# RWKV-5 attention and a SwiGLU block on one core: part of the input loads begun by ScalarE instead of SyncE

## The chip, the core and the metric

The kernel runs on one core of a Trainium2 chip. The metric is the time of one execution on the device in microseconds (us). The engines are called PE (TensorE, with PEld for its weight loads), DVE (VectorE), ACT (ScalarE), POOL (GpSimd) and SP (SyncE). SP computes nothing here: it begins transfers (DMAs). ACT computes, and it can begin transfers too; a transfer that an engine begins stands in that engine's instruction stream, in order with the rest of it. Such an instruction is called an issue below; the time at which all its data have arrived is its landing.

## What is computed

Inputs are r, k, v of shape (4 batches, 8 heads, 768 steps, 48), w and u of shape (8, 48), and the weights of the second part in float64, which the kernel reads as pairs of 32-bit words and rounds itself. All else is float32.

```python
for t in range(S):                                   # first part, by batch and head
    kt, vt, rt = (k[:, :, t], v[:, :, t], r[:, :, t])
    cur = np.einsum('bhd,bhe->bhde', u[None] * kt, vt)
    y[:, :, t] = np.einsum('bhd,bhde->bhe', rt, state + cur)
    state = w[None, :, :, None] * state + np.einsum('bhd,bhe->bhde', kt, vt)
x = y.transpose(0, 2, 1, 3).reshape(B * S, H * D)    # (3072, 384)
g = x @ w_gate                                       # w_gate, w_val: (384, 1536)
out = (g * (1.0 / (1.0 + np.exp(-g))) * (x @ w_val)) @ w_out
```

## The kernel before

**Units.** The first part is cut into 24 units, each worth 128 steps of all 8 heads. Units 0 to 7 are 128 steps of one batch; from unit 8 (`PAIRED`) on a unit holds 64 steps of each of two batches, in the two halves of the partitions. A loop over s runs unit s+1's preparation, unit s-1's scores and unit s-2's outputs side by side, and fills the gaps with matmuls of the second part (`feed`). Per unit: `load` brings k and r (two DMAs, four from unit 8 on, L147), `load_v` brings v (L153); POOL scales k and r and forms their product (L353, L356, L264, L267); unit 8 and later move 32-wide blocks inside SBUF with eight DMAs of SP (`move_blocks`, L435), which DVE transposes (L457); PE makes the scores (L496, later L548); DVE copies them under a mask into the tile At (L504, later L556); ACT writes the diagonal (L384, later L376 into a side tile that two of ACT's own DMAs bring into At, `fill_own`, L532); SP brings the transposed r there too (`fill_turned`, L526). PE multiplies At by v (L647, later L582) and ACT copies the result to xT (L651, later L586).

**Weights.** `chunks` lists 18 pieces of the weights, 0 to 17, in this text called chunks: 0 to 11 take turns between w_gate and w_val, 12 to 17 are w_out. `load_weights` (L184) begins the load of the next one into `w_bits`, a ring of three buffers of 768 KB. A chunk is then rounded to float32, by ACT (two L204 and one L210, in the order L204, L210, L204), DVE (L219 and L220 twice) and POOL (L252). `round_second` ends a chunk's rounding on ACT and begins a load, so that chunk n+2's load is written down right behind chunk n's rounding. PE uses rounded gate and value weights for units 0 to 3 while the rest is still being rounded (L690; ACT's L696 and DVE's L697 take its results from two PSUM banks); w_out must be complete before the first projection (L770). Later PE works on sums of weights that POOL forms (L862, L889, L959).

**Order.** The framework keeps each engine's instructions in the order in which the kernel writes them. It gives each transfer begun by SP or ACT one of eight completion counters, DMAHW0 to DMAHW7, in turn, both engines' transfers in one sequence; a transfer waits, before it is issued, for the landing of the last one that had its counter, which is the eighth before it in that sequence. Where the two are on different engines, one engine's stream stands until the other's transfer has landed.

Of the kernel before, what the change touches and what calls it, by code (L numbers as in the profile page):

```python
# [22 lines left out]
def fast(  # L23
# [25 lines left out]
    B, H, S, D = r.shape  # L49
# [15 lines left out]
    dve, pool, act, pe, sp = nc.vector, nc.gpsimd, nc.scalar, nc.tensor, nc.sync  # L65
# [63 lines left out]
    PAIRED = 8  # L129
# [6 lines left out]
    def pieces_of(i):  # L136

        if i < PAIRED:
            c, b = divmod(i, B)
            return [(slice(0, P), b, P * c)]  # L140
        return [(slice(64 * p, 64 * p + 64), *part(i, p)) for p in range(2)]
# [7 lines left out]
    def load_v(i):  # L149
        for rows, b, t in pieces_of(i):  # L150
            n = rows.stop - rows.start
            for e in range(2):
                sp.dma_start(  # L153
                    out=v_ld[b][rows, :, 64 * e : 64 * e + D],
                    in_=v[b, :, t : t + n, :].rearrange("(a e) t d -> e t a d", e=2)[e],
                )
# [17 lines left out]
    def next_chunk(stage):  # L174
        n = done[stage]
        done[stage] = min(n + 1, NW)
        return n if n < NW else None

    def load_weights():
        n = next_chunk("load")  # L180
        if n is not None:
            src = chunks[n][0].bitcast(INT32)
            bits[n] = three.tile([P, WN, 2], INT32, name="w_bits", tag="w_bits")
            sp.dma_start(  # L184
                out=bits[n][:].rearrange("p (c f) two -> p c (f two)", c=src.shape[1]), in_=src
            )

# [47 lines left out]
    def round_second(n):  # L235
        round_high(n, 1, 1)
        round_dve(n, 1)
        del bits[n]
        load_weights()
# [54 lines left out]
    load(0)  # L294
    load(1)
    load_weights()
    load_weights()
    load_v(0)
    load_v(1)

    act.activation(sg0[:], ident[:, 0:1], AF.Silu)
# [25 lines left out]
    for l in range(7):  # L327
        n = 1 << l
# [1054 lines left out]
    load(3)  # L1383
    load_weights()
    load_v(2)
    load_v(3)
    scores(0)
# [162 lines left out]
    n = nc.values_load(outside, min_val=0, max_val=512)  # L1550
# [416 lines left out]
```

## Time and profile before

| | |
|---|---|
| median of 3 runs | 609.83 us (606.59 to 610.46) |
| the profiled execution | 608.74 us, of which its span is 606.9 us |
| PE busy | 571.4 us, 94% of the span |
| DVE, POOL, ACT busy | 434.1, 393.2 and 221.2 us |
| moved by DMA | 51.26 MB |
| mean granted PE clock | 0.977 of full speed |

The span is what the profile's times count from; 1.8 us of the execution lie outside it. The chain of waits is read back from the last instruction: each row is the work that released the next. A row of the timeline gives start, duration, engine and line, and in brackets how long the engine stood idle before and what ended that; "SPq" and "ACTq" mark an issue in the stream of SP or ACT. A row of the waits gives the total, how often, and the longest.

### The profile page before, as it was taken

What the parts mean: (1) busy time and instruction counts of PE and PEld (TensorE: products, weight loads), DVE (VectorE), ACT (ScalarE), POOL (GpSimd) and SP (SyncE); (2) the same over time, 40 slices, a digit from 0 to 9 for tenths busy, and PEclk for the clock granted to TensorE, in tenths of its full rate; (3) what the DMA queues carried; (4) which work ended last, traced back from release to release, by engine and by line L of the source; (5) the groups of instructions that cost most, each with busy time, mean ns of one, the idle gap of its engine ahead of it and who ended that gap; (6) DMA issues with size and microseconds to landing.
All of it is one profiled execution on the core that took longest, in us unless ns stands there. A gap on an engine that the chain in (4) does not pass through costs nothing.

```text
span 606.9 us, 13839 instructions
## 1 busy us (share of the span) xinstructions
PE 571.4 (94%) x5450; PEld 513.8 (85%) x5450; DVE 434.1 (72%) x766; ACT 221.2 (36%) x528; POOL 393.2 (65%) x394
## 2 busy tenths in 40 slices
PE   8899959396999999999999999999999999999997
PEld 6788847285997889998889998889988889988896
DVE  7977666348748787959778959769728779367682
ACT  4669654221134443134452135441133331133320
POOL 5898756468699983797963797952998980001520
PEclk9999978599999999999999999999999999999999
DMA  7997968466354332564441564241110000200002
GB/s 194 222 261 207 230 198 157 114 123 106 65 116 78 71 65 45 91 138 74 81 78 32 115 124 73 44 75 29 28 27 0 1 2 1 53 0 2 1 2 56
DMA packets 161912, 51.26 MB, mean 84 GB/s; under 512 B 148465, under 2 KB 151538, under 8 KB 161842
## 3 DMA queue, kind: packets, MB, share of 16 engines
q1 hardware_dynamic: 156690, 42.79, 34.0%
q10 hardware_dynamic: 5152, 7.54, 4.9%
q8 instruction: 44, 0.72, 0.5%
q14 instruction: 26, 0.21, 0.1%
HBM read 28.31 MB, written 4.72 MB: 54 GB/s over the span
## 4 chain that ended last, share of the span: by engine, by line
PE 75%; DMA 7%; POOL 7%; SPq 3%; DVE 2%; issue 2%; ACT 2%; POOLq 0%; DVEq 0%; ACTq 0%
PE bank L959 28%; PE bank L770 14%; PE ring L959 13%; PE bank L1192 8%; PE bank L690 5%; DMA w_bits<-in_moe_w_out_dram 4%; POOL wgv L862 3%; PE ring L582 3%; POOL s L889 2%; PE ring L548 1%; DMA v_ld<-in_v_dram 1%; PE ring L1192 1%; PE ring L647 1%; DMA w_bits<-in_moe_w_val_dram 1%; PE ring L596 1%
## 5 line engine op out<-in xcount | busy, mean ns | idle before, releaser
L983 DVE TENSOR_TENSOR hv<-hv,bank 128x512 f32<-128x512 f32 x132 | 87.8, 683 | 37.5 <-PE bank L959 31.8
L690 PE MATMUL bank<-xT,wgv 128*128 128x256 f32 x288 | 69.3, 398 | 6.9 <-DVE hv L697 6.9
L690 PEld LDWEIGHTS bank<-xT,wgv 128*128 128x128 f32 x288 | 55.8, 198 | 16.1 <-DVE hv L697 7.3
L959 PE MATMUL bank<-xf,wgv 128*128 128x256 f32 x256 | 65.6, 381 | 0.0
L983 ACT COPY hv<-bank 128x512 f32<-128x512 f32 x72 | 40.8, 585 | 61.8 <-PE bank L959 54.4
L959 PEld LDWEIGHTS bank<-xf,wgv 128*128 128x128 f32 x256 | 48.1, 190 | 6.8 <-DVE kT L1237 0.6
L1246 POOL TENSOR_TENSOR hv<-At,hats 128x512 f32<-128x512 f32 x8 | 10.2, 1275 | 64.0 <-ACT At L1245 64.0
L376 ACT ACTIVATE zs<-mask,du 128x64 f32<-128x64 f32 x128 | 38.8, 345 | 26.4 <-DVE du L275 10.4
L990 ACT ACTIVATE hv<-hv 128x512 f32<-128x512 f32 (+2 forms) x36 | 22.8, 634 | 50.2 <-DVE hv L983 50.2
L770 PE MATMUL bank<-wt,hs 128*128 128x192 f32 x192 | 35.5, 338 | 4.1 <-DVE hs L744 4.1
L615 POOL TENSOR_TENSOR v_ld<-v_ld,w 48x384 f32<-48x384 f32 x28 | 24.4, 871 | 19.1 <-DVE v_ld L612 16.0
L770 PEld LDWEIGHTS bank<-wt,hs 128*128 128x128 f32 x192 | 32.9, 197 | 4.5 <-POOL rk L267 4.3
L959 PE MATMUL bank<-xT,wgv 128*128 128x256 f32 x144 | 35.6, 380 | 0.0
L959 PE MATMUL bank<-xT,s 128*128 128x256 f32 x152 | 35.4, 381 | 0.0
L889 POOL TENSOR_TENSOR s<-wgv 128x256 f32<-128x256 f32 x39 | 29.9, 787 | 7.3 <-PE bank L770 7.3
L770 PE MATMUL bank<-wo,hv 128*128 128x192 f32 x192 | 32.9, 327 | 1.7 <-DVE hv L697 1.7
L770 PE MATMUL bank<-wo,hs 128*128 128x192 f32 x192 | 34.0, 327 | 0.0
L770 PEld LDWEIGHTS bank<-wo,hv 128*128 128x128 f32 x192 | 31.5, 190 | 2.4 <-DVE hv L697 2.0
L959 PEld LDWEIGHTS bank<-xT,s 128*128 128x128 f32 x152 | 28.5, 190 | 4.8 <-issue 1.1
L747 POOL TENSOR_TENSOR hs<-hv,hs 128x768 f32<-128x768 f32 x6 | 11.3, 1876 | 32.1 <-DVE hs L744 32.1
L889 POOL TENSOR_TENSOR s<-s,wgv 128x256 f32<-128x256 f32 x39 | 30.2, 774 | 2.8
L889 POOL TENSOR_TENSOR s<-s 128x256 f32<-128x256 f32 x39 | 31.5, 806 | 0.8
(237 smaller groups left out, 1424.3 us busy)
## 6 DMA issues: line engine op xcount, KB each, us to landing
hats<-hats SPq DMA_DIRECT2D x128, 64.0 KB, 2.3
w_bits<-in_moe_w_gate_dram SPq DMA_DIRECT2D x6, 768.0 KB, 6.4
w_bits<-in_moe_w_val_dram SPq DMA_DIRECT2D x6, 768.0 KB, 7.2
w_bits<-in_moe_w_out_dram SPq DMA_DIRECT2D x6, 768.0 KB, 6.0
At<-zs ACTq DMA_DIRECT2D x32, 128.0 KB, 3.3
At<-rT SPq DMA_DIRECT2D x32, 128.0 KB, 2.4
k_ld<-in_k_dram SPq DMA_DIRECT2D x32, 96.0 KB, 3.3
r_ld<-in_r_dram SPq DMA_DIRECT2D x32, 96.0 KB, 3.1
```

The source lines that it names most:

```text
L376: lambda h=h: act.activation(own[:, i % 2, slot(i, h), :], ident64, AF.Identity, scale=du[:, h : h + 1])
L582: pe.matmul(ps[32 * q : 32 * q + 32, cc, 64 * p : 64 * p + 64], *x, start=start, stop=stop, skip_group_check=True,)
L615: pool.tensor_mul(ze, ze, w.unsqueeze(3).to_broadcast([D, HP, 2, D]))
L690: pe.matmul(gv[:, o, :].rearrange("p (i t) -> p i t", i=2), wt[:, c, P * f : P * (f + 1)], xT[:, 2 * g % NX : 2 * g % NX + 2, c, :], start ...
L747: on.tensor_sub(s[1], h12, x["s"][1])
L770: pe.matmul(ps, lhs[:, f, :], rhs[:, f, :], start=(f == 0 and n in (0, 1, 4)), stop=(f == FH - 1), skip_group_check=True,)
L862: lambda o=o, x=x, op=op: op(o, o, x) for o, x, op in ((w[1][1], w[0][1], pool.tensor_add), (w[1][1], w[1][2], pool.tensor_sub), (w[0][0], ...
L889: op(made[o], made[a], made[b])
L959: pe.matmul(ps[:, o], u[:, o], v, start=first and o == 0, stop=True, skip_group_check=True,)
L983: do(out, *(pair_of(wide[a][:]) if isinstance(a, str) else a for a in args))
L990: todo.append((at, lambda: act.activation(gate, gate, AF.Silu)))
L1192: pe.matmul(ps, (h[what][q] if h[what] is D_ else h[what][:, q])[:, f, :], wide["o"][what][:, f, :], start=first and f == 0 and (split or ...
```

## The change

Two lines change which engine begins a transfer. Chunk 5 and later are loaded by ACT (`n < 5` stays on SP; chunk 5 is the sixth), and so is v for units 8 to 11. What is moved, to where and how much stays the same.

```diff
@@ -150,7 +150,7 @@
         for rows, b, t in pieces_of(i):
             n = rows.stop - rows.start
             for e in range(2):
-                sp.dma_start(
+                (act if PAIRED <= i < PAIRED + B else sp).dma_start(
                     out=v_ld[b][rows, :, 64 * e : 64 * e + D],
                     in_=v[b, :, t : t + n, :].rearrange("(a e) t d -> e t a d", e=2)[e],
                 )
@@ -181,7 +181,7 @@
         if n is not None:
             src = chunks[n][0].bitcast(INT32)
             bits[n] = three.tile([P, WN, 2], INT32, name="w_bits", tag="w_bits")
-            sp.dma_start(
+            (sp if n < 5 else act).dma_start(
                 out=bits[n][:].rearrange("p (c f) two -> p c (f two)", c=src.shape[1]), in_=src
             )
```

So 13 issues of weights and 16 of v (four for each of four units) leave SP's stream and stand in ACT's. The orders of PE, DVE and POOL do not change.

ACT, from the end of chunk 4's rounding (rows of before with -, of the change with +, and in brackets the counters that a row waits for):

```order
+L184 DMA w_bits<-in_moe_w_gate_dram 128x3x512 [waits DMAHW7_49,Activation_49]
 L409 COPY kT_112<-ring_96 128x512 [waits PE_49]
 L409 COPY rT<-ring_97 128x512 [waits PE_49]
-L204 ACTIVATE bank_94<-w_bits 128x384 [waits DMAHW4_49,DVE_49]
-L210 ACTIVATE w_low<-w_bits 128x768 [waits Pool_49]
-L204 ACTIVATE bank_95<-w_bits 128x384 [waits DVE_49]
+L204 ACTIVATE bank_94<-w_bits 128x384 [waits DVE_49]
+L210 ACTIVATE w_low<-w_bits 128x768 [waits Pool_49]
+L204 ACTIVATE bank_95<-w_bits 128x384 [waits DVE_49]
+L184 DMA w_bits<-in_moe_w_val_dram 128x3x512 [waits DMAHW4_49,Activation_49]
 L696 ACTIVATE sgs<-bank_92 128x256 [waits PE_49]
 L384 ACTIVATE At_110<-ident,du 128x128 x3
```

The loads of chunks 6 and 7 now stand behind the rounding of chunks 4 and 5, and ACT's next work stands behind the loads. Chunk 7's load has counter DMAHW4, whose last user before it is on SP. There, in the changed kernel, stand the loads of k and r for unit 7 (k_ld_104, r_ld_102):

```order
L153 DMA v_ld_106<-in_v_dram 128x4x48 [waits DMAHW1_49,PE_49]
L153 DMA v_ld_106<-in_v_dram 128x4x48 [waits DMAHW2_49,PE_49]
L147 DMA k_ld_104<-in_k_dram 128x8x48 [waits DMAHW3_49,Pool_49]
L147 DMA r_ld_102<-in_r_dram 128x8x48 [waits DMAHW4_49]
L1464 DMA w_82<-w_82 64x4x1 [waits DMAHW5_49]
L1464 DMA w_82<-w_82 64x4x1 [waits DMAHW6_49]
```

So ACT's load of chunk 7 waits until r of unit 7 has landed; in the kernel before, that load stood on SP behind r's issue.

SP before, where it begins the load of the last chunk, 17 (the only L184 here), between the loads of k and r for unit 11 and those of v for unit 9:

```order
L147 DMA k_ld_104<-in_k_dram 64x8x48 [waits DMAHW3_49]
L147 DMA k_ld_104<-in_k_dram 64x8x48 [waits DMAHW4_49]
L147 DMA r_ld_102<-in_r_dram 64x8x48 [waits DMAHW5_49]
L147 DMA r_ld_102<-in_r_dram 64x8x48 [waits DMAHW6_49]
L184 DMA w_bits<-in_moe_w_out_dram 128x2x768 [waits DMAHW7_49,Activation_49]
L677 DMA v_ld_108<-zs 48x4x48 [waits DMAHW0_49,PE_49,Pool_49]
L677 DMA v_ld_108<-zs 48x4x48 [waits DMAHW1_49,PE_49,Pool_49]
L153 DMA v_ld_107<-in_v_dram 64x4x48 [waits DMAHW2_49]
```

In the changed kernel the L184 and the L153 are gone from this place. The chunk's load now stands on ACT behind chunk 15's rounding, with counter DMAHW2. ACT in the changed kernel, from chunk 16's rounding on (v_ld_107 and v_ld_108 are the v of unit 9):

```order
L204 ACTIVATE bank_94<-w_bits 128x384 [waits DMAHW6_49,DVE_49]
L210 ACTIVATE w_low<-w_bits 128x768 [waits Pool_49]
L204 ACTIVATE bank_95<-w_bits 128x384 [waits DVE_49]
L376 ACTIVATE zs<-mask,du 128x64 x2
L651 COPY xT<-ring_96 128x384 [waits PE_49]
L532 DMA At_111<-zs 64x512 [waits DMAHW7_49,Activation_49]
L532 DMA At_111<-zs 64x512 [waits DMAHW0_49]
L153 DMA v_ld_107<-in_v_dram 64x4x48 [waits DMAHW2_49]
L153 DMA v_ld_107<-in_v_dram 64x4x48 [waits DMAHW3_49]
L153 DMA v_ld_108<-in_v_dram 64x4x48 [waits DMAHW5_49,PE_49]
L153 DMA v_ld_108<-in_v_dram 64x4x48 [waits DMAHW6_49,PE_49]
L696 ACTIVATE sgs<-bank_92 128x256 [waits PE_49]
```

Before, the L696 stood right behind the two L532. Now the four issues of v stand between them, and the first of these, which has DMAHW2 too, waits until chunk 17 has landed.

## The prediction

> **What bounds the kernel now.** First the span, then stages of it, since the change touches only the first 140 us. In a row of stages stand the bounds and the length, each engine's busy us, the granted PE clock, the share in which DMA engines were busy, and GB/s.
>
> ```profile
> span 606.9 us, 13839 instructions
> ...
> core 0: us, PE busy (x) PEld busy (x) DVE busy (x) ACT busy (x) POOL busy (x), PEclk, DMA share, GB/s
> 36.00:58.00 22.00, 22.00 (x214) 19.17 (x213) 16.54 (x35) 18.98 (x48) 19.93 (x18) 1.00 0.91 230
> 58.00:82.00 24.00, 23.81 (x291) 20.34 (x289) 14.96 (x31) 14.21 (x34) 18.92 (x17) 1.00 0.85 202
> 82.00:117.00 35.00, 17.08 (x198) 14.03 (x202) 20.90 (x42) 17.81 (x49) 16.66 (x15) 0.73 0.63 153
> 117.00:133.00 16.00, 15.18 (x276) 13.08 (x268) 6.05 (x14) 4.01 (x13) 11.17 (x8) 0.85 0.68 128
> ...
> 150.00:194.00 44.00, 43.23 (x462) 39.97 (x461) 31.11 (x55) 11.19 (x31) 36.66 (x45) 0.97 0.43 86
> ```
>
> PE is full from 36 to 82 and again from 150 on. Between 82 and 117 it works 17.08 of 35.00 us. So **no engine bounds that stage; a chain of waits does**. The longest waits of PE and one of SP's stream (total, count, longest), then the chain of waits there:
>
> ```profile
> PE ring L582 <- DVE At L556: 11.2, 1, 11.2
> PE bank L690 <- DVE hv L697: 6.9, 1, 6.9
> ...
> SPq L147 <- DMA At<-zs: 13.0, 5, 5.5
> ```
>
> ```profile
> 91.50 5.92 DMA w_bits<-in_moe_w_out_dram
> ...
> 99.81 2.92 DMA At<-zs
> 102.75 0.65 SPq L147
> ...
> 104.12 0.63 SPq L147
> 104.85 6.63 DMA w_bits<-in_moe_w_out_dram
> ...
> 115.97 0.45 DVE At L556
> 116.46 0.55 PE ring L582 x12
> ```
>
> PE's longest wait ends at 116.46 (that for L697 lies ahead of it in the same stage). Read backwards: L582 waits for the mask copy At (DVE, 115.97). Ahead of it stands chunk 17's rounding, which waits for that chunk's load. The load was issued only at 104.85, because SP was standing before k of unit 11 (102.75), which needed a counter from ACT's At<-zs (99.81 + 2.92 = 102.73). SP stood 13.0 us in five such places. ACT's own timeline shows the other end:
>
> ```profile
> 94.78 0.52 ACT L204 ACTIVATE bank<-w_bits 128x384 f32<-128x384 f32 x1
> ...
> 97.50 0.54 ACT L204 ACTIVATE bank<-w_bits 128x384 f32<-128x384 f32 x1 [1.18 <-DMA w_bits<-in_moe_w_out_dram]
> ...
> 99.81 1.18 ACTq L532 DMA_DIRECT2D At<-zs  x2
> 101.04 0.38 ACT L696 ACTIVATE sgs<-bank 128x256 f32<-128x256 f32 x1 [0.89 <-ACT xT L651]
> 103.17 0.83 ACT L376 ACTIVATE zs<-mask,du 128x64 f32<-128x64 f32 x3 [1.74 <-DVE du L275]
> 111.50 0.51 ACT L204 ACTIVATE bank<-w_bits 128x384 f32<-128x384 f32 x1 [7.50 <-DMA w_bits<-in_moe_w_out_dram]
> ```
>
> Chunk 15's rounding ends at 95.30 (94.78 + 0.52), and behind it stands chunk 17's load in the changed kernel: 9.5 us earlier than 104.85. Chunk 17 is rounded at 111.50, after 7.50 us of standing, and PE resumes 4.96 us later.
>
> **Prices.** Issues on SP, what two issues cost ACT (the bracket of 101.04), and landings:
>
> ```profile
> 41.19 0.57 SPq L147 DMA_DIRECT2D r_ld<-in_r_dram  x1
> ...
> 67.12 1.32 SPq L147 DMA_DIRECT2D r_ld<-in_r_dram  x2
> ...
> 104.85 0.57 SPq L184 DMA_DIRECT2D w_bits<-in_moe_w_out_dram  x1
> ...
> 127.70 2.64 SPq L153 DMA_DIRECT2D v_ld<-in_v_dram  x4
> ...
> 130.43 1.23 SPq L526 DMA_DIRECT2D At<-rT  x2
> ```
>
> ```profile
> DMA to landing us min/median/max: 5.1/6.4/7.6
> ```
>
> ```profile
> DMA to landing us min/median/max: 2.6/3.2/6.6
> ```
>
> The first landing row is L184 in the whole trace, the second L147. ACT has no row of a weight load. Its two L532, 1.18 us of issue, held the next instruction 0.89 us, 0.45 each; its computing rows overlap by about 0.1 us. So a load costs ACT between nothing (under a wait) and 0.57; I take **0.3**, and **2.6** for four v issues (2.64 on SP). A load's landing on ACT's queue is bounded by 5.1 and 7.6; I take **5.6**, between the least and the 5.92 of chunk 16, which had fewer transfers around it than the median of 6.4.
>
> **The change, step by step.** Shifts are times after minus before.
>
> *Chunk 7's load (36 to 58).* It takes the counter of r of unit 7, so ACT waits for a landing of SP.
>
> ```profile
> DMA to landing us min/median/max: 5.7/5.8/5.9
> ```
>
> These are the k and r loads issued about 35, in the same traffic. 41.19 + 5.8 = 47.0, against 43.1 where chunk 5's rounding ends; with 0.3 and the overlap, L696 of 42.99 comes at 47.4: +4.4. By the median of 3.2 it would be 44.4 + 0.3, by the 6.6 it would be 47.8 + 0.3, so +1.7 to +5.1. ACT idles later:
>
> ```profile
> 42.99 0.38 ACT L696 ACTIVATE sgs<-bank 128x256 f32<-128x256 f32 x1
> ...
> 50.12 0.53 ACT L204 ACTIVATE bank<-w_bits 128x384 f32<-128x384 f32 x1 [0.53 <-DVE wgv L220]
> ...
> 58.62 0.38 ACT L696 ACTIVATE sgs<-bank 128x256 f32<-128x256 f32 x1 [0.78 <-PE bank L690]
> ...
> 65.77 0.54 ACT L204 ACTIVATE bank<-w_bits 128x384 f32<-128x384 f32 x1 [2.08 <-DMA w_bits<-in_moe_w_gate_dram]
> ...
> 69.10 0.53 ACT L204 ACTIVATE bank<-w_bits 128x384 f32<-128x384 f32 x1 [0.58 <-DMA w_bits<-in_moe_w_val_dram]
> ...
> 82.30 0.51 ACT L204 ACTIVATE bank<-w_bits 128x384 f32<-128x384 f32 x1 [4.61 <-DMA w_bits<-in_moe_w_out_dram]
> 87.79 0.38 ACT L696 ACTIVATE sgs<-bank 128x256 f32<-128x256 f32 x1 [0.89 <-ACT xT L651]
> ```
>
> 4.4 less 0.53, 0.78 and 2.08, plus 0.3 for each of four loads (chunks 8 to 11), is +2.2 at chunk 10's rounding (68.0); less 0.58, plus a load, +1.9 at chunk 11's (71.0). PE reads L696's bank and may stop some 2 us in this stage. I count that at nothing: PE idles 17.9 of the 35.00 us from 82 on, where this work can stand. Without that cover it would be +2.
>
> *Chunk 13's load.* It takes the counter of the first r half of unit 10, issued at 67.12. SP is some 4.4 late there, as its stream waits for counters of ACT's loads: 71.5 + 3.2 = 74.7, landing 80.3. Chunk 13 is rounded at 80.3 instead of 82.30: −2.0.
>
> *v of unit 8.* These four stand behind the L532 ahead of 87.79. From chunk 13 at 80.3 to this L696 ACT needs 5.49 as before, plus a load (0.3) and the v (2.6): 88.7, **+0.9**. Chunk 15's rounding then ends at 96.2.
>
> *Chunk 17 and v of unit 9.* Chunk 16's rounding stays at 97.5: its load, begun about 91, lands about 97. Chunk 17 is issued at 96.2 and lands at 101.8. The first v of unit 9 has its counter, so ACT stands behind the L532 until 101.8, then issues until 104.4: L696 of 101.04 moves by +3.4. What is queued behind: L376 (103.17), which waits for a DVE product written behind the multiplication that this L696 feeds; it comes at 106.6, ends at 107.4, and chunk 17's rounding follows there instead of 111.50: **−4.1**. PE resumes at 112.4.
>
> *v of units 10 and 11.* SP's four issues at 127.70 go.
>
> ```profile
> 128.16 0.70 DVE L457 STREAM_TRANSPOSE rT<-hats 128x512 f32<-128x512 f32 x1
> ...
> 139.65 0.71 DVE L457 STREAM_TRANSPOSE kT<-hats 128x512 f32<-128x512 f32 x1 [1.49 <-DMA hats<-hats]
> ```
>
> L526 at 130.43 reads rT, ready at 128.86; its start and the moves behind it come up to 1.57 us earlier, and kT at 139.65 waited 1.49 for them. I take half, **−0.8**; bounds 0 and −1.5. On ACT the issues lie in its idle time (it is busy 4.01 of 16.00 there).
>
> *Sum.* −4.1 − 0.8 = −4.9. From 150 on PE is full, and what starts earlier there ends earlier. The profiled execution is 608.74: 608.74 − 4.9 = **603.8**; it lies 1.1 below the median of 609.83, against which the forecast is −1.0%.
>
> **Rivals.** *The waits are short (better).* If chunk 7's wait ends at 44.4 and landings take 5.1, chunk 13's stage keeps its −2.0 and v of unit 9 starts 1 to 2 us earlier: round 17 at about 105.5, −6. PE's idle stretch gets short enough that part of the clock loss goes: 117 to 133 has 0.85 on 15.18 busy us, 2.3 us of work lost, and at most the whole is won. With −1.5 and −2.3: 608.74 − 6 − 3.8 = 599, to 597 with chunk 15 earlier as well. For it speaks that most of ACT's rows have slack; against it, that SP's r of unit 7 is issued in a stage with 0.91 DMA share.
>
> *Nothing to gain (neutral).* The 16 DMA engines are busy 0.85 and 0.63; if the load of chunk 17 started at 96.2 is itself slowed by the v, k and r around it to end about 106, as its rows of 7.6 begin to show, chunk 17 is rounded at about 111.5 and only 0 to 0.8 is won: 608 to 609. Against it: chunk 17's lost time was 9.5 us of waiting to be issued, against 6.63 us of transfer. The Trainium skill, DMA: Bandwidth & Descriptors, section "Issuing engines are not separate DMA queues", speaks for this rival: transfers begun by scalar, sync or gpsimd run on the same 16 DMA engines and interleave, and several issuers save only sequencer time, "usually small relative to the DMA itself". By that rule the time would stay at 608 to 609; the chain's rows disagree at this one place, where SP's stream was not issuing but standing.
>
> *ACT is blocked (slower).* The waits for counters stand in front of ACT's compute now. With landings of 7.6 on ACT's queue and 47.8 at chunk 7: chunk 13 issued 75.5, landed 83.1, chunk 15 landed 92.4, L696 at 93.1 (+5.3); chunk 17 issued at 100.6, landed 108.2, v issued to 110.8, chunk 17 rounded at 113.8, +2.3: **611.0**. It decides at a landing of about 7.1, as each us of landing costs 3.2 (three loads in a row): (113.8 − 107.4) / (7.6 − 5.6). For it: the row of landings has 7.6, and a wait of PE's in 36 to 58 could add its 2 us: 613. Against it: chunks 16 and 17 took 5.92 and 6.63 beside SP's traffic.
>
> **How the numbers follow.** My forecast case 0.50, with 600.5 to 607 of its own (the bounds of kT, of the loads' price and landings of 5.1 to 6.5); better 0.15, neutral 0.18, slower 0.17. The range of 8 in 10 takes in half of the better case and most of the slower one: 597.5 to 612. A measurement of this kernel can tell about 1%, 6.1 us, from no change. Under 603.7 lie the better case and about half of the forecast's: faster 0.42. Above 615.9 only the blocked case in a worse form, and delays of PE between 36 and 82 that I took as covered: 0.14. Within 1%: 0.44.
>
> **What would show it.** In the profile after: the load of chunk 17 as an ACTq row near 96; the first v of unit 9 behind it near 102 with DMA w_bits as releaser; L204 of chunk 17 near 107 and PE's L582 near 112; an ACTq row of chunk 7 near 47 released by r_ld; no L153 of SP near 128. I am wrong if PE stops more than 3 us between 36 and 82, if ACT's landings are far from 5.6, or if the steps behind 117 do not follow L582: kT at 139.65 may wait for something that does not move.

## The result and the profile after

The changed kernel takes **612.83 us** (median of 11 runs) against 608.65 (11 runs): ratio 1.0068, 95% interval 1.0042 to 1.0093. It is slower by 0.7%, where 1% faster was forecast. The profiled execution took 611.44 us, its span is 609.6.

First the stages of the profile after, with the same columns as before:

```profile
36.00:58.00 22.00, 20.25 (x172) 17.05 (x174) 14.04 (x29) 16.40 (x42) 17.21 (x16) 1.00 0.94 234
58.00:82.00 24.00, 23.56 (x331) 20.47 (x320) 17.46 (x36) 16.83 (x41) 20.11 (x19) 1.00 0.80 199
82.00:117.00 35.00, 18.69 (x199) 15.16 (x201) 20.99 (x43) 17.80 (x49) 17.88 (x16) 0.83 0.70 157
117.00:133.00 16.00, 14.17 (x239) 11.97 (x239) 6.27 (x15) 4.00 (x13) 10.01 (x8) 0.85 0.66 122
```

PE now stops between 36 and 58 (20.25 of 22.00 us). Between 82 and 117 it works 18.69 us, 1.6 more than before, so work was put off, as forecast; but the chain through that stage does not end earlier. The waits show where the standing went (total, count, longest):

```profile
ACT sgs L696 <- DMA v_ld<-in_v_dram: 17.6, 4, 5.0
...
PE bank L690 <- DVE hv L697: 12.7, 3, 10.0
...
PE ring L582 <- DVE At L556: 4.8, 2, 3.8
```

PE's wait for the mask copy fell from 11.2 to 4.8 us, and that for L697 rose from 6.9 to 12.7. L697 takes what L696 made, and L696 now stands behind the issues of v: 17.6 us in four places. Most of the first two (3.90 and 3.74 us, 0.89 each before) is new; at the other two, L696 of 123.80 and of 135.19, ACT waited 5.08 and 4.52 us for PE before. ACT's timeline, at the rows that the prediction walked through:

```profile
45.52 0.38 ACTq L184 DMA_DIRECT2D w_bits<-in_moe_w_val_dram  x1
45.94 0.38 ACT L696 ACTIVATE sgs<-bank 128x256 f32<-128x256 f32 x1 [2.77 <-DMA r_ld<-in_r_dram]
...
76.69 0.39 ACTq L184 DMA_DIRECT2D w_bits<-in_moe_w_out_dram  x1
77.12 0.48 ACT L651 COPY xT<-ring 128x384 f32<-128x384 f32 x1 [4.32 <-DMA r_ld<-in_r_dram]
...
82.42 0.53 ACT L204 ACTIVATE bank<-w_bits 128x384 f32<-128x384 f32 x1 [0.78 <-DMA w_bits<-in_moe_w_out_dram]
...
87.92 2.02 ACT L376 ACTIVATE zs<-mask,du 128x64 f32<-128x64 f32 x8 [3.12 <-DMA v_ld<-zs]
...
91.18 2.98 ACTq L153 DMA_DIRECT2D v_ld<-in_v_dram  x4
94.20 0.38 ACT L696 ACTIVATE sgs<-bank 128x256 f32<-128x256 f32 x1 [3.90 <-DMA v_ld<-in_v_dram]
...
99.24 0.38 ACTq L184 DMA_DIRECT2D w_bits<-in_moe_w_out_dram  x1
...
106.16 2.83 ACTq L153 DMA_DIRECT2D v_ld<-in_v_dram  x4
109.03 0.39 ACT L696 ACTIVATE sgs<-bank 128x256 f32<-128x256 f32 x1 [3.74 <-DMA v_ld<-in_v_dram]
111.14 0.83 ACT L376 ACTIVATE zs<-mask,du 128x64 f32<-128x64 f32 x3 [1.73 <-DVE du L275]
111.88 0.49 ACT L204 ACTIVATE bank<-w_bits 128x384 f32<-128x384 f32 x1
```

Chunk 17 is loaded 5.6 us earlier (99.24 against 104.85), and its rounding has no bracket any more: ACT did not wait for the load. Yet it begins at 111.88, 0.4 us later than before, because ACT itself arrived only then. In front of it stand two stops for r (2.77 and 4.32), one for zs (3.12) and two rows of v issues (2.98 and 2.83).

Behind that stage another 1.15 us is lost, as the L586 that ends the next block shows, before and after:

```profile
130.19 0.48 ACT L586 COPY xT<-ring 128x384 f32<-128x384 f32 x1 [0.36 <-PE ring L582]
```

```profile
131.72 0.48 ACT L586 COPY xT<-ring 128x384 f32<-128x384 f32 x1 [1.68 <-PE ring L582]
```

The chain of waits there, in the profile after:

```profile
120.27 4.70 DMA v_ld<-in_v_dram
124.98 0.59 SPq L435
...
125.62 2.31 DMA hats<-hats
...
128.15 0.71 DVE kT L457
```

The last moves of hats (L435) stand on SP until v of unit 10, issued by ACT from 120.27 on, has landed; no data tie the two, so what they share is a counter. DVE's transpose waits for the hats, and L586 comes at +1.53, of which 0.38 was there at chunk 17. The last part lies in PE's block behind its idle time, which ends at 149.57 before and at 150.96 after. The stretch that starts there, before and after:

```profile
149.50:153.50 4.00, 3.92 (x35) 3.73 (x38) 3.97 (x4) 0.22 (x1) 3.84 (x4) 0.61 0.43 70
```

```profile
151.00:155.50 4.50, 4.50 (x29) 4.06 (x33) 4.43 (x5) 0.32 (x1) 4.34 (x4) 0.50 0.41 73
```

At a granted clock of 0.50 instead of 0.61, PE takes 4.18 us for the 12 matmuls that open this block (3.67 before) and 1.54 for the L582 behind them (1.11 before), and the next L586 (154.35 before) is at +2.3 us. From there on the shift stays. This last part was not tried on its own; in the kernel without chunk 7 on ACT, tried below, it is missing (−0.66 us at the one L586, −0.51 at the next).

### The profile page after: what moved, and what is told of

It reads as the page before. It is cut to its first block, busy times and chain, and to the rows that moved or that the text cites. A ratio compares the mean times of both kernels' runs of the same rounds, so it can differ in the third digit from the quotient of the medians.

```text
span 609.6 us, 13830 instructions
## 1 busy us (share of the span) xinstructions
PE 572.2 (94%) x5450; PEld 513.9 (84%) x5450; DVE 434.2 (71%) x766; ACT 220.8 (36%) x528; POOL 392.4 (64%) x394
## 4 chain that ended last, share of the span: by engine, by line
PE 76%; DMA 6%; POOL 6%; DVE 5%; ACT 3%; SPq 1%; issue 1%; ACTq 0%; DVEq 0%; POOLq 0%
PE bank L959 28%; PE bank L770 17%; PE ring L959 13%; PE bank L1192 8%; PE bank L690 3%; PE ring L582 3%; DMA v_ld<-in_v_dram 2%; DMA hats<-hats 2%; PE ring L548 2%; POOL s L889 1%; PE ring L1192 1%; DMA v_ld<-zs 1%; PE ring L596 1%; PE ring L647 1%; ACT zs L376 1%
## 5 line engine op out<-in xcount | busy, mean ns | idle before, releaser
L690 PE MATMUL bank<-xT,wgv 128*128 128x256 f32 x288 | 68.5, 393 | 12.7 <-DVE hv L697 12.7
L376 ACT ACTIVATE zs<-mask,du 128x64 f32<-128x64 f32 x128 | 38.7, 344 | 29.2 <-DVE du L275 9.9
L747 POOL TENSOR_TENSOR hs<-hv,hs 128x768 f32<-128x768 f32 x6 | 11.2, 1874 | 32.1 <-DVE hs L744 32.1
```

The source lines that it names most:

```text
L376: lambda h=h: act.activation(own[:, i % 2, slot(i, h), :], ident64, AF.Identity, scale=du[:, h : h + 1])
L690: pe.matmul(gv[:, o, :].rearrange("p (i t) -> p i t", i=2), wt[:, c, P * f : P * (f + 1)], xT[:, 2 * g % NX : 2 * g % NX + 2, c, :], start ...
L747: on.tensor_sub(s[1], h12, x["s"][1])
```

## The experiments

Each kernel differs from the kernel before only in the two lines of the change. "Here" in the table is the median, and the ratio is to runs of the kernel before on the same chip. There are 6 to 12 runs of each kernel and one profile. Ahead of the first change, rows of these profiles already differ by up to 0.9 us, and the profiled execution need not be a typical one: that of the weights alone took 609.55 us, in a kernel whose runs go from 602.56 to 609.86. So prices are read from the ratios, and the profiles say where the time went.

| on ACT | here, us | ratio | 95% interval |
|---|---|---|---|
| chunks 5 to 17 and v (the change) | 612.83 | 1.0068 | 1.0042 to 1.0093 |
| chunks 5 to 17 | 607.24 | 0.9965 | 0.9937 to 0.9993 |
| v of units 8 to 11 | 615.41 | 1.0104 | 1.0074 to 1.0134 |
| chunk 17 | 604.95 | 0.9938 | 0.9910 to 0.9966 |
| chunks 5 to 17, v of 10 and 11 | 607.84 | 0.9982 | 0.9960 to 1.0005 |
| chunks 14 to 17 | 603.19 | 0.9919 | 0.9894 to 0.9943 |
| chunks 5 to 17 without 13 | 606.98 | 0.9982 | 0.9962 to 1.0002 |
| chunks 16 and 17 | 601.88 | 0.9888 | 0.9864 to 0.9911 |
| chunks 8 to 17 | 602.71 | 0.9911 | 0.9878 to 0.9944 |
| the change without chunk 7 | 608.88 | 1.0000 | 0.9976 to 1.0024 |
| chunk 7 | 608.07 | 0.9986 | 0.9970 to 1.0002 |
| chunks 16 and 17, v of 8 and 9 | 606.35 | 0.9972 | 0.9946 to 0.9998 |
| chunks 5 to 7 | 611.13 | 1.0047 | 1.0024 to 1.0070 |

### Weights alone, v alone, chunk 17 alone

Weights alone:

```diff
@@ load_weights, L184
-            sp.dma_start(
+            (sp if n < 5 else act).dma_start(
```

> Weights of chunks 5 to 17 on ACT as in the change, all v back on SP. Theory A (the change's gain is eaten by v: eight of ACT's v issues, 2.98 and 2.83 us, stand ahead of the L696 that gate chunks 14 to 17, and eight later ones let SP's block moves wait for v's landings): chunk 17 is rounded 2.8 to 5.8 us earlier than the 111.88 of the change, the step of 1.15 us at 129.8 goes, and the time is 3 to 6 us under before, 603 to 606. Rival B (what costs is the weights: ACT waits for SP's k, r and zs transfers ahead of chunks 7, 12 and 13): no faster than before, 608 to 612.

v alone:

```diff
@@ load_v, L153
-                sp.dma_start(
+                (act if PAIRED <= i < PAIRED + B else sp).dma_start(
```

> v of units 8 to 11 on ACT, all weights back on SP. A: L696 of 101.04 and its chain come some 3 us later, SP's load of chunk 17, which waits for ACT's L532, 2 to 4 us later than 104.85, and the step of 1.15 stays: 610.5 to 614. B: v on ACT is hidden in ACT's idle time, 607 to 610.

Chunk 17 alone:

```diff
@@ load_weights, L184
-            sp.dma_start(
+            (sp if n < 17 else act).dma_start(
```

> Only chunk 17 is loaded by ACT, all else by SP as before. If the wait for chunk 17's issue is what sets the stage's end (my forecast's step): the load is issued near 95.3, lands near 101.5, chunk 17 is rounded near 104 instead of 111.50, and the time is 4 to 7 us under before, 602 to 605. If the transfer is only slowed (the DMA engines' rival): issued early, but landed past 106, and 607 to 609.

Chunk 17 alone gives 0.62%: the step of the forecast on which the gain rested is right. Its load and its rounding in that kernel, where ACT's wait for a load of 7.50 us before is gone:

```profile
92.85 0.48 ACTq L184 DMA_DIRECT2D w_bits<-in_moe_w_out_dram  x1
...
103.65 0.51 ACT L204 ACTIVATE bank<-w_bits 128x384 f32<-128x384 f32 x1
```

103.65 against 111.50 is 7.9 us, and the load was not slowed: it landed 4.7 us after its issue. v alone costs 1.04%, a little over the upper end of what the theory expected. In its profile the two rows of v issues are there, and ACT still waits for chunk 17, whose load SP begins later than before:

```profile
87.97 3.22 ACTq L153 DMA_DIRECT2D v_ld<-in_v_dram  x4
...
103.24 3.02 ACTq L153 DMA_DIRECT2D v_ld<-in_v_dram  x4
...
114.69 0.51 ACT L204 ACTIVATE bank<-w_bits 128x384 f32<-128x384 f32 x1 [5.45 <-DMA w_bits<-in_moe_w_out_dram]
```

Weights alone come out between the two expectations: faster than before by 0.35%, but by 0.27% less than chunk 17 alone (the intervals of these two overlap). So v explains most of the loss, and something in the earlier chunks the rest.

### v of units 10 and 11, and of 8 and 9

```diff
@@ load_v, L153
-                sp.dma_start(
+                (act if PAIRED + 2 <= i < PAIRED + B else sp).dma_start(
@@ load_weights, L184
-            sp.dma_start(
+            (sp if n < 5 else act).dma_start(
```

> The change with v of units 8 and 9 back on SP, so that only units 10 and 11 have their v on ACT. A: chunk 17's rounding as in the kernel with weights alone on ACT, and after it the step of 1.1 to 1.5 at the mask copy L556 of unit 10 as in the change: 604 to 607, 1 to 1.5 above weights alone. B: 609 to 612, as the change.

```diff
@@ load_v, L153
-                sp.dma_start(
+                (act if PAIRED <= i < PAIRED + 2 else sp).dma_start(
@@ load_weights, L184
-            sp.dma_start(
+            (sp if n < 16 else act).dma_start(
```

> Chunks 16 and 17 on ACT, and v of units 8 and 9 as well; all else on SP. A (v's issues ahead of L696 cost what they last, twice 2.9 us, since ACT's chain sets the end of the stage now): chunk 17's rounding 4 to 6 us later than the 102.1 of chunks 16 and 17 alone, 605.5 to 608. B (hidden in ACT's idle time): 601 to 603.

The first is 0.17% above weights alone, 1.0 us by the ratios and 0.6 by the medians: the right direction, but within the intervals; its median of 607.84 lies just above the range given. The second costs 0.84% over chunks 16 and 17 alone, with intervals apart (0.9864 to 0.9911 against 0.9946 to 0.9998). In that kernel no SP load of chunk 17 is in the way, so this is the price of v in front of ACT's chain. Its rows, and behind them the rounding of chunk 17 with chunks 16 and 17 alone:

```profile
88.30 3.20 ACTq L153 DMA_DIRECT2D v_ld<-in_v_dram  x4
...
103.60 2.81 ACTq L153 DMA_DIRECT2D v_ld<-in_v_dram  x4
106.46 0.38 ACT L696 ACTIVATE sgs<-bank 128x256 f32<-128x256 f32 x1 [3.75 <-DMA v_ld<-in_v_dram]
...
109.31 0.50 ACT L204 ACTIVATE bank<-w_bits 128x384 f32<-128x384 f32 x1
```

```profile
102.08 0.50 ACT L204 ACTIVATE bank<-w_bits 128x384 f32<-128x384 f32 x1
```

Two rows of 3.20 and 2.81 us, and chunk 17's rounding 7.2 us later in these profiles, more than the 4 to 6 expected; the 0.84% are 5.1 us. So hardly any of the 6.0 us of v issue is hidden.

### Which of the earlier chunks costs

```diff
@@ load_weights, L184
-            sp.dma_start(
+            (sp if n < 14 else act).dma_start(
```

> Chunks 14 to 17 on ACT, the rest and all v on SP. If what costs in the weights alone is the traffic and the counters of chunks 5 to 13 (r of unit 10 landing 6.7 us after its issue beside chunk 12's load, ACT standing 3.7 to 4.3 us for it ahead of chunk 13), nothing of it is here: no ACT row waits for r_ld, and the time is that of chunk 17 alone, 602 to 606. If chunks 14 and 15 beside SP's zs transfers are what costs (ACT's L376 waits 3 to 6 us for v_ld<-zs), the wait shows here too and the time is 606 to 609.

```diff
@@ load_weights, L184
-            sp.dma_start(
+            (sp if n < 5 or n == 13 else act).dma_start(
```

> Weights of chunks 5 to 17 on ACT except chunk 13, which SP loads; all v on SP. If ACT's standing for r of unit 10 ahead of chunk 13's load is the main loss of the weights: the 3.7 us are gone, 603.5 to 605.5. If the loss is the slower landing of SP's small transfers beside ACT's loads, wherever the wait shows: 606 to 609, as weights alone.

```diff
@@ load_weights, L184
-            sp.dma_start(
+            (sp if n < 16 else act).dma_start(
```

> Chunks 16 and 17 on ACT, the rest and all v on SP. Chunk 16 is issued behind chunk 14's rounding, near 90 instead of 91.5, so that the 1.0 to 1.2 us that ACT waits for it at 97.5 go: 601 to 605, at most 1 us under chunk 17 alone. If the two loads only share the DMA engines: the same as chunk 17 alone, 603 to 606.

```diff
@@ load_weights, L184
-            sp.dma_start(
+            (sp if n < 8 else act).dma_start(
```

> Chunks 8 to 17 on ACT, the rest and all v on SP: chunk 7's load waits for nothing on ACT. If the stop of PE between 36 and 58 (2.7 us of idle time in the kernel with weights alone) is made up later, as I forecast: 606 to 609, as weights alone. If it is kept to the end: 603.5 to 605.5.

Chunks 8 to 17, 14 to 17 and 16 and 17 lie close together (0.9911, 0.9919, 0.9888), with intervals that overlap. Chunks 14 and 15 do seem to cost a little: on one chip all six runs of 16 and 17 (600.93 to 602.56 us) lie under all six of 14 to 17 (602.81 to 604.87). The runs of 8 to 17 (599.92 to 605.87) cannot be told from either. So chunks 8 to 13 cost little if anything, which speaks against the theory that the traffic and counters of chunks 12 and 13 make the loss, although ACT's stop for r ahead of chunk 13, 5.01 us, stands in the profile of chunks 8 to 17 as well (first row below). In the kernel with 5 to 17 but without 13 that stop was gone and replaced: ACT then waited 8.84 us for chunk 13 itself, which SP began behind its block moves (second row).

```profile
75.83 0.48 ACT L651 COPY xT<-ring 128x384 f32<-128x384 f32 x1 [5.01 <-DMA r_ld<-in_r_dram]
```

```profile
87.33 0.51 ACT L204 ACTIVATE bank<-w_bits 128x384 f32<-128x384 f32 x1 [8.84 <-DMA w_bits<-in_moe_w_out_dram]
```

So that kernel's time, 606.98, falls in the second of the two expected ranges, but because of this new wait, and it does not settle what chunk 13's stop costs. What remains is chunks 5 to 7: leaving them on SP is worth 0.54% (0.9965 to 0.9911; the intervals overlap a little), and the 602.71 of chunks 8 to 17 is below both of its expected ranges. In its profile PE does not stop between 36 and 58, but it stops in the next stage, where the kernel with the weights alone works 23.58 us:

```profile
36.00:58.00 22.00, 22.00 (x214) 19.17 (x213) 16.54 (x34) 18.91 (x47) 19.90 (x17) 1.00 0.95 239
58.00:82.00 24.00, 21.83 (x275) 18.83 (x274) 15.90 (x33) 15.56 (x37) 18.41 (x17) 0.93 0.78 205
```

So a stop of PE in these stages does not by itself cost time at the end.

### Chunk 7

```diff
@@ load_v, L153
-                sp.dma_start(
+                (act if PAIRED <= i < PAIRED + B else sp).dma_start(
@@ load_weights, L184
-            sp.dma_start(
+            (sp if n < 5 or n == 7 else act).dma_start(
```

> The change with chunk 7 alone loaded by SP again (v of units 8 to 11 and all other chunks from 5 on stay on ACT). Theory C (ACT's stop for r of unit 7 ahead of chunk 7's load is not made up: it moves POOL's and SP's work into the landings of chunks 14 and 15): the stop of PE between 36 and 58 and ACT's wait for zs before L376 are gone, 3 us or more come back, 606 to 610. Rival D (what chunks 8 to 17 alone gain over chunks 5 to 17 comes from chunks 5 and 6): as the change, 611 to 614.

```diff
@@ load_weights, L184
-            sp.dma_start(
+            (act if n == 7 else sp).dma_start(
```

> Only chunk 7 on ACT, all else as before. C: L696 of 42.99 comes 2.5 to 3.8 us later and PE stops for about 2.5 us; if that alone carries to the end, 610.5 to 612. If the slack in ACT and PE takes it up by 82, as I forecast, and it costs only beside later loads on ACT: 607.5 to 609.5, with chunk 17 rounded at 111.5 as before.

```diff
@@ load_weights, L184
-            sp.dma_start(
+            (act if n in (5, 6, 7) else sp).dma_start(
```

> Chunks 5, 6 and 7 on ACT, all else as before. Chunk 7's load takes the counter of r of unit 7 here, as in the change, which it did not in the kernel with chunk 7 alone on ACT, so ACT stands and L696 of 42.99 comes near 46. If that stop carries to the end by itself: 610.5 to 612.5. If it is made up where SP's chain sets the later stage, and costs only with later loads on ACT: 607 to 609.5.

The change without chunk 7 is 0.68% faster than the change (608.88 against 612.83, intervals apart): one load of 18. Theory C held on the time, but not on all it said: ACT's wait for zs ahead of L376 is still there (3.57 us), so in this kernel something other than chunk 7's stop brings that wait about.

Chunk 7 alone did not test the stop. In that kernel ACT issues the load at 42.01 without standing; the transfer that had its counter before had landed:

```profile
42.01 0.47 ACTq L184 DMA_DIRECT2D w_bits<-in_moe_w_val_dram  x1
```

It shows that the issue as such costs nothing that can be measured (0.9986). With chunks 5 to 7 on ACT, chunk 7 meets r of unit 7 again, the rest is as before, and 0.47% is lost. The chain of waits of this kernel tells how:

```profile
41.19 4.97 DMA r_ld<-in_r_dram
...
46.24 0.39 ACTq L184
...
46.67 0.38 ACT sgs L696
...
63.15 6.34 DMA w_bits<-in_moe_w_gate_dram
...
72.76 6.64 DMA w_bits<-in_moe_w_out_dram
...
81.37 5.19 DMA w_bits<-in_moe_w_out_dram
...
95.83 5.63 DMA w_bits<-in_moe_w_out_dram
...
103.86 3.04 DMA At<-zs
...
109.02 5.87 DMA w_bits<-in_moe_w_out_dram
```

L696 comes at 46.67, 3.7 us later than 42.99, and every later load in this chain is late by about as much or more: chunk 12 issued at 72.76 instead of 68.54, chunk 16 at 95.83 instead of 91.50, chunk 17 at 109.02 instead of 104.85. ACT waits for a load in five places of this kernel, yet the 3.7 us are not made up: each load, begun by SP only behind an earlier rounding on ACT, is late with it.

## Why the prediction was wrong, step by step

The median lies 9.0 us above the forecast of 603.8. Two steps carry most of that: a stop of ACT that was put at nothing, and the covers under which v was to be hidden.

**Chunk 17 (right).** Its late issue set the end of the stage, and bringing it to ACT takes 7.9 us off its rounding where nothing else is moved. The neutral rival, for which the prediction cites the Trainium skill, DMA: Bandwidth & Descriptors, section "Issuing engines are not separate DMA queues", is contradicted in this case: one load begun by the other engine saves 0.62%. The saved time is not that of issuing, which the section speaks of, but of standing in a stream.

**"I count that at nothing" (the first step that failed).** The stop at chunk 7 was rightly foreseen: L696 at 45.94, +2.95 (forecast +4.4, bounds 1.7 and 5.1). The forecast then let it run off in ACT's later idle times, 0.53, 0.78 and 2.08 us, and in PE's idle time after 82, as if all of these were slack. ACT in the changed kernel at these three places:

```profile
53.04 0.52 ACT L204 ACTIVATE bank<-w_bits 128x384 f32<-128x384 f32 x1 [0.56 <-DVE wgv L220]
...
61.42 0.38 ACT L696 ACTIVATE sgs<-bank 128x256 f32<-128x256 f32 x1 [0.66 <-PE bank L690]
...
66.48 0.54 ACT L204 ACTIVATE bank<-w_bits 128x384 f32<-128x384 f32 x1
```

The first two, waits for DVE and PE, moved along with ACT (+2.92 and +2.80) and took up next to nothing. Only the 2.08 us, a wait for chunk 10's load, was slack: its rounding is at +0.71, where +2.2 was forecast. But ACT then stands for r of unit 10, and chunk 12's rounding, 74.65 before, is at 78.64. With chunks 5 to 7 alone on ACT even the wait for chunk 10's load is kept, and its rounding is at +3.80:

```profile
69.57 0.55 ACT L204 ACTIVATE bank<-w_bits 128x384 f32<-128x384 f32 x1 [2.36 <-DMA w_bits<-in_moe_w_gate_dram]
```

PE did make up work after 82, 1.6 us of it, but the stage ends behind ACT's roundings and not behind PE's work. The stop costs 0.47 to 0.68%, 2.9 to 4.1 us of 608.7, by three pairs of kernels; only the pair with 0.68% moves chunk 7 alone. With chunks 5 to 7 alone the profile shows the way to the end: loads that set out behind late roundings. In the changed kernel it is open in part. There, taking chunk 7 off ACT makes ACT's rows 3.5 us earlier at the stop, 1.4 at chunk 17's rounding and 2.9 at the L586 of 154.35 before.

**v (the second step that failed: mis-sized).** The price of one row was about right, 2.98 and 2.83 us against 2.6. But I let the second row lie half under the wait for chunk 17's landing, and the first under chunk 13's earlier rounding. Neither cover was there: chunk 17's load did not hold v's issue (106.16 stands directly behind the two L532), and chunk 13's rounding was not earlier (82.42 against 82.30). Four pairs of kernels with and without v on ACT differ by 0.84% (units 8 and 9 only), 0.89% (a pair that differs in chunks 5 and 6 too), 1.03% and 1.04%, 5.1 to 6.3 us, where the forecast had 5.2 us of issues in ACT's stream and, by the covers, a shift of 3.4 at the second L696.

**Chunk 13 (mis-sized).** Forecast issue 74.7 and rounding 80.3; it was issued at 76.69 and rounded at 82.42, because r of unit 10, issued at 69.92 and so earlier than the 71.5 of the forecast, took 6.7 us to land and not 3.2:

```profile
DMA to landing us min/median/max: 6.7/6.7/6.7
```

I had taken the median of all of SP's k and r loads, in a row whose largest value is 6.6. Chunk 13's own landing, 5.6 us, was as forecast.

**The wait for zs (missed).** L376 stood 3.12 us, since it overwrites what SP's L677 was still reading; SP began the two L677 in question at 80.02 and 81.78, where it had begun them at 77.97 and 78.7. With it, L696 behind v of unit 8 came at 94.20 where I had 88.7: 2.1 from chunk 13, 3.1 from zs, 0.4 from v.

**SP's gain of 0.8 (wrong sign).** SP's four issues of v went, but its moves then waited for the landing of the same v on ACT: kT came at 141.04 and not before 139.65. That is the third of the signs of being wrong that the prediction named; the other two did not show, as PE stopped 2.2 us and not 3 between 36 and 82, and ACT's landings are near 5.6.

The rival that came closest is the blocked ACT, with 611.0 and L696 at 93.1; its condition, landings of 7.6, was not met (chunk 13 took 5.7 from its issue to its rounding). ACT was blocked by counters, by zs and by v's issues, not by slow landings of its own loads. That the time comes near this rival's is luck.

By parts, along one path of kernels: chunks 16 and 17 alone −1.12%; chunks 8 to 15 as well +0.23 (within the intervals); 5 to 7 as well +0.54; v as well +1.03; together the +0.68 measured. These are differences of ratios, each with an interval of its own of some 0.3 either way. The fastest of the kernels tried is chunks 16 and 17 on ACT, 601.88 us.

## What to carry to other kernels

A transfer moved to an engine that computes brings its waits along: look up which earlier transfer has its counter, and ask which compute stands behind it. Idle time of an engine is slack only if what ends it does not itself depend on that engine; where it waits for loads that its own work sets off, a delay runs through. Move the one transfer whose late issue the chain names, and leave the others.

## What the runs showed of the hardware beyond that

Beside the 768 KB load of chunk 12, which ACT had issued at 68.98, SP's r of unit 10 landed 6.7 us after its issue. In the kernel before, the landings of such loads that anything waited for took 2.6 to 6.6 us, with a median of 3.2; so this is the upper end of what was there already. The zs transfer that ACT's L376 waited for took 6.04, in this row of the chain of the changed kernel:

```profile
81.78 6.04 DMA v_ld<-zs
```

Before, the zs transfers issued from 87.27 on took 5.6 to 6.1, so this one was not slower than those; it was begun later. Whether loads on ACT's queue slow SP's small transfers is not shown: no run took the loads away from beside these transfers alone.
